# Transfers of keys and of split values in a top-k attention with two MoE layers: begun by ScalarE's queue in place of SyncE's

## The chip, the cores and the metric

The kernel runs on one core of a Trainium2 chip. The metric is the device time of one execution in microseconds; lower is better. Names of engines in the profile: PE is TensorE (PEld its weight loads), DVE is VectorE, ACT is ScalarE, POOL is GpSimd, and SPq is the queue of SyncE, which computes nothing and only begins transfers.

## What is computed

An attention that keeps the 32 largest scores of each row, and two MoE-like layers behind it, all in float32 accuracy.

```python
batch, n_heads, seq, head_dim = (4, 8, 576, 64)
scores = scale * np.matmul(q, k.transpose(0, 1, 3, 2))
kth = np.partition(scores, -top_k, axis=-1)[..., -top_k:-top_k + 1]   # top_k = 32
scores = np.where(scores >= kth, scores, -1000000000.0)
attn = softmax(scores)                                                 # + 1e-9 in the divisor
x = np.matmul(attn, v)            # to 2304 tokens x 512
x = (sigmoid(x @ w_gate) * (x @ w_val)) @ w_out      # 512 -> 1536 -> 512
out = np.maximum(x @ w_in, 0) ** 2 @ w_out2          # 512 -> 2048 -> 512
```

## The kernel before

The 2304 tokens are 18 tiles of 128 rows; `CHUNKS` makes 12 chunks of them: chunks 0 to 5 of one tile, chunks 6 to 11 of two. A sequence has 576 rows, so a tile can lie in two batches (then two key tiles are needed). Within a chunk the attention goes over four pairs of heads (`hp`), two heads (`j`) and the tiles (`i`); one such unit is: queries transposed, `scores` (L374, TensorE, into `sp`), a copy of them to SBUF by ScalarE (`S`, L377), four rounds of the eight largest by VectorE (L389, L396), the exponential by ScalarE (L408 to L424), and the product with the values.

For the accuracy, operands are split into a high and a low part. `prep_keys` reads the keys of a batch and a pair of heads, transposes them, casts the high part `kp` (L172, ScalarE), takes the low part `kn` (L173, VectorE) and stores both to a scratch tensor `ks` in HBM (L179, SyncE). `load_keys` (L326) fetches from there the 128 x 576 tile `kst` that a head needs; the pool has `KST` = 3 buffers for `kst`, and `kp` takes one of the same three. A buffer is free when the matmuls of the unit that read it are done.

From chunk 6 (`TCI`) on, values are split too: `prep_values` and `split_values` store them to the scratch `vd` (L229, L230), and `load` fetches `v` (L308) from it, into one of two buffers, free when the product `xp` of the earlier pair is done. Chunks 0 to 5 load plain values (L314, L317). From chunk 6 on the probabilities are transposed by a transfer, `PT<-S` (L456). Queries come by L298, outputs leave by L893. All these transfers are begun by SyncE, one after the other in one queue: an issue whose buffer isn't free holds up all that stand behind it.

The MoE layers of a chunk run on TensorE between the units of later chunks: pg and pv (L749), acc (L789), ph (L853), acc (L874). ScalarE, GpSimd and VectorE work on their results in between (th, gh, r, rh); the PSUM pool for pg, pv and ph has two buffers. For chunks 0 and 1 the same is done in float32 with lines of its own.

The order on every engine comes from a scheduler that gets the instructions with priorities (`tc.high_priority`, `at`, `attend`) and puts them in an order by its own plan of the time. The order is then fixed: each engine takes its instructions one by one and waits at each for what it needs. A change of one instruction's engine can therefore move others.

Of the kernel before, what the change touches and what calls it, by code (L numbers as in the profile page):

```python
# [10 lines left out]
F32 = mybir.dt.float32  # L11
# [33 lines left out]
XP = (0, 1)  # L45
CN = 16
CA2 = 5.0
SM2 = ()
XUP = 1000
DIAG = 2  # L50
# [24 lines left out]
def tile_topk_attention__then__two_moe_layers(  # L75
# [14 lines left out]
    nc = tc.nc  # L90
# [52 lines left out]
    kscr = {}  # L143
# [40 lines left out]
    vscr = {}  # L184
# [49 lines left out]
    def pieces(tt):  # L234
        r0, r1 = tt * P, (tt + 1) * P
        res = []
        while r0 < r1:
            b = r0 // S
            e = min(r1, (b + 1) * S)
            res.append((b, r0 - b * S, r0 - tt * P, e - r0))  # L240
            r0 = e
        return res
# [39 lines left out]
    class Pair:  # L282
# [9 lines left out]
        def load(self):  # L292
            ci, hp = self.ci, self.hp
            for tt in self.tts:
                qn = apool.tile([P, 2, 2, D], F32, tag="qn", bufs=2, name=f"qn_{tt}_{hp}")
                for b, s0, o, n in pieces(tt):
                    for a in range(2):
                        nc.sync.dma_start(  # L298
                            qn[o : o + n, :, a, :],
                            q[b, 2 * hp : 2 * hp + 2, s0 : s0 + n].rearrange("h p d -> p h d"),  # L300
                        )
                self.qt[tt] = qn
            for b, _, _ in self.segs:
                if ci >= TCI:
                    t = apool.tile(
                        [P, 2, 2, CB + 1, D], F16, tag="v", bufs=2, name=f"v_{ci}_{hp}_{b}"
                    )
                    nc.sync.dma_start(t, vscr[(b, hp)])  # L308
                    self.vt[b] = t
                    continue  # L310
                t = apool.tile([P, 2 * CB + 1, D], F32, tag="v", bufs=2, name=f"v_{ci}_{hp}_{b}")
                src = v[b, 2 * hp : 2 * hp + 2]
                for j in range(2):
                    nc.sync.dma_start(  # L314
                        t[:, j * CB : (j + 1) * CB], src[j, 0:SM].rearrange("(p c) d -> p c d", c=CB)
                    )
                    nc.sync.dma_start(t[j * ST : (j + 1) * ST, 2 * CB], src[j, SM:S])  # L317
                self.vt[b] = t

        def load_keys(self, j):  # L320
            h = 2 * self.hp + j
            if self.ci == 0:
                return
            for b, _, _ in self.segs:
                t = apool.tile([P, S], F32R, tag="kst", bufs=KST, name=f"kst_{self.ci}_{h}_{b}")
                nc.sync.dma_start(t.bitcast(F32), kscr[(b, h)].bitcast(F32))  # L326
                self.kt[(j, b)] = t

        def queries(self, tts):
# [676 lines left out]
    def attention():  # L1006
# [62 lines left out]
        def tail(n, after=None):  # L1069
# [3 lines left out]
            if pr.hp == 0 and pr.ci not in xts:  # L1073
# [10 lines left out]
                else:  # L1084

                    small = pr.ci in SM2
                    x = mpool.tile(
# [102 lines left out]
    for ci in PLAIN:  # L1190
        n = 0
        while True:
# [28 lines left out]
            else:  # L1221
                at(ta)
                with tc.high_priority(offset=0):
                    if next(att, 1) is None:
                        emitted[0] += 1
                ta += CA if emitted[0] < CN else CA2
        body = None
# [56 lines left out]
```

## Time and profile before

| | |
|---|---|
| median of three runs | 1276.93 us (1275.36 to 1278.46) |
| profiled execution | 1279.16 us |
| its span, first to last instruction | 1277.4 us |
| mean granted clock of TensorE | 0.955 of full speed |
| busy: PE, DVE, ACT, POOL | 93%, 75%, 65%, 66% |
| transfers of `kst` | 112 of 288 KB |
| transfers of split `v` | 32 of 320 KB |

A page and views of one profiled execution follow below as rows. A group of waits sums the idle time of an engine in front of an instruction by what ended it (the releaser, behind the arrow). A stretch gives the busy time of each engine in it, with the number of instructions in brackets. Busy time of an engine doesn't count the issuing of transfers. A granted clock of 1.00 is 2.4 GHz on TensorE, the lower level is 1.2 GHz; a mean between them says for what part of the stretch the lower one held.

### The profile page before, as it was taken

The numbers are of one execution on the slowest core, as the hardware profiler recorded it, in microseconds if no ns is written. First come the engines' busy times: TensorE is split into PE (matmuls) and PEld (weight loads), VectorE is DVE, ScalarE is ACT, GpSimd is POOL, SyncE is SP. The second block draws the span as 40 slices with busy tenths as digits, with TensorE's granted clock in tenths as the row PEclk, the third lists the DMA queues.
The fourth block names the chain that finished last, engine by engine and source line by source line (L and its number), as shares of the span: only waits on it lengthen the run. The fifth ranks groups of instructions, "written<-read, shape, count | busy, mean of one in ns | idle before, by whom it ended". The sixth has DMA issues, their size and how long they took to land.

```text
span 1277.4 us, 30680 instructions
## 1 busy us (share of the span) xinstructions
PE 1186.4 (93%) x11477; PEld 963.2 (75%) x11477; DVE 955.9 (75%) x1965; ACT 832.1 (65%) x1719; POOL 837.7 (66%) x1294
## 2 busy tenths in 40 slices
PE   6767989999889898999998999999999999999998
PEld 5556877987877877879786768877886887787775
DVE  6998888999778967889998779989989969210010
ACT  4998986677767666767777666777677757323122
POOL 1788864577766476787876877797778649515223
PEclk9567989999989998999998999999999999999999
DMA  7987862223344336765676656556444523200000
GB/s 189 352 301 258 272 193 77 75 79 84 103 131 125 104 80 144 143 151 115 143 135 158 119 131 143 129 113 162 105 82 96 120 48 67 55 1 1 17 1 18
DMA packets 243190, 153.94 MB, mean 121 GB/s; under 512 B 193120, under 2 KB 209504, under 8 KB 243040
## 3 DMA queue, kind: packets, MB, share of 16 engines
q1 hardware_dynamic: 243040, 151.97, 46.9%
q8 instruction: 91, 1.49, 0.5%
q14 instruction: 59, 0.48, 0.1%
HBM read 105.51 MB, written 18.09 MB: 97 GB/s over the span
## 4 chain that ended last, share of the span: by engine, by line
PE 64%; DVE 11%; DMA 8%; POOL 6%; ACT 5%; issue 3%; SPq 2%; POOLq 0%; DVEq 0%; ACTq 0%
PE ph L853 10%; PE acc L874 10%; PE pg L749 8%; PE pv L749 7%; PE acc L789 7%; PE sp L374 6%; DVE mx L389 5%; DVE W L396 4%; PE xp L506 3%; DMA PT<-S 3%; PE ph L954 2%; PE xp L533 2%; PE acc L971 2%; PE pg L907 2%; DMA kst<-ks 2%
## 5 line engine op out<-in xcount | busy, mean ns | idle before, releaser
L389 DVE MAX8 mx<-W 128x8 f32<-128x576 f32 x432 | 327.8, 759 | 10.8
L396 DVE MATCH_REPLACE8 W<-mx,W 128x576 f32<-128x576 f32 x288 | 213.8, 743 | 0.0
L853 PE MATMUL ph<-x,wi_w 128*128 128x256 f16 (+1 forms) x1920 | 193.0, 255 | 2.5 <-ACT x L827 1.9
L874 PE MATMUL acc<-w_w,rh 128*128 128x512 f16 x768 | 181.6, 379 | 3.2 <-POOL rh L866 3.1
L853 PEld LDWEIGHTS <-wi_w 128*128 128x128 f16 x1920 | 158.3, 100 | 29.1 <-issue 3.0
L749 PE MATMUL pg<-xs,wg_w 128*128 128x256 f16 (+1 forms) x1440 | 150.0, 256 | 3.5 <-ACT xs L520 2.8
L374 PE MATMUL sp<-kst,qt 128*128 128x288 f32 x608 | 135.7, 336 | 18.0 <-DMA kst<-ks 9.3
L749 PE MATMUL pv<-xs,wv_w 128*128 128x256 f16 (+1 forms) x1440 | 145.2, 254 | 4.8 <-DVE th L761 4.3
L377 ACT COPY S<-sp 128x576 f32<-128x576 f32 x144 | 91.9, 638 | 71.8 <-PE sp L374 42.5
L454 POOL TENSOR_TENSOR S<-W,S 128x512 f16<-128x512 f32 x192 | 136.7, 733 | 2.0
L749 PEld LDWEIGHTS <-wv_w 128*128 128x128 f16 x1440 | 118.7, 99 | 21.0 <-issue 8.4
L749 PEld LDWEIGHTS <-wg_w 128*128 128x128 f16 x1440 | 120.4, 100 | 18.4 <-issue 2.0
L408 ACT ACTIVATE W<-S,mx 128x576 f32<-128x576 f32 x144 | 111.6, 775 | 30.4 <-DVE mx L389 29.8
L874 PEld LDWEIGHTS <-rh 128*128 128x128 f16 x768 | 72.4, 98 | 75.4 <-POOL rh L866 4.0
L789 PEld LDWEIGHTS <-wo_w 128*128 128x128 f16 x1440 | 117.8, 98 | 13.6 <-issue 1.4
L761 DVE TENSOR_TENSOR th<-pv,th 128x512 f32<-128x512 f32 (+1 forms) x60 | 34.6, 577 | 121.5 <-PE pv L749 118.9
L389 DVE MAX8 mx<-S 128x8 f32<-128x576 f32 x144 | 107.3, 745 | 24.1 <-ACT S L377 24.1
L374 PEld LDWEIGHTS sp<-kst,qt 128*128 128x128 f32 x608 | 93.5, 198 | 29.3 <-DMA kst<-ks 9.7
L452 POOL TENSOR_SCALAR W<-W,rz 128x576 f32<-128x576 f32 x96 | 71.5, 745 | 66.8 <-ACT S L451 65.6
L865 POOL TENSOR_TENSOR r<-r 128x512 f32<-128x512 f32 (+1 forms) x80 | 69.5, 868 | 59.7 <-ACT rh L864 58.5
L396 DVE MATCH_REPLACE8 W<-mx,S 128x576 f32<-128x576 f32 x144 | 106.9, 742 | 0.0
L789 PE MATMUL acc<-gh,wo_w 128*128 128x256 f16 (+1 forms) x1104 | 105.0, 247 | 0.9 <-POOL gh L765 0.9
(290 smaller groups left out, 2324.1 us busy)
## 6 DMA issues: line engine op xcount, KB each, us to landing
kst<-ks SPq DMA_DIRECT2D x112, 288.0 KB, 3.1
v<-vd SPq DMA_DIRECT2D x32, 320.0 KB, 3.6
qn<-in_q_dram SPq DMA_DIRECT2D x128, 64.0 KB, 2.5
wi_r<-in_moe_w_in_dram SPq DMA_DIRECT2D x16, 512.0 KB, 6.5
w_r<-in_moe_w_out_dram SPq DMA_DIRECT2D x16, 512.0 KB, 5.2
v<-in_v_dram SPq DMA_DIRECT2D x56, 128.0 KB, 2.3
wg_r<-in_moe_w_gate_dram SPq DMA_DIRECT2D x12, 512.0 KB, 6.3
wv_r<-in_moe_w_val_dram SPq DMA_DIRECT2D x12, 512.0 KB, 6.8
```

Of the source, the lines that this page charges most:

```text
L374: nc.tensor.matmul(sp[:, e, 0:HALF], l, r, start=(x == 0), stop=(x == len(ops) - 1))
L377: nc.scalar.copy(ss.rearrange("p (e s) -> p e s", e=2), sp[:, :, 0:HALF])
L389: m8 = nc.vector.max(mx[:, r], cur)
L396: nc.vector.match_replace(wk, mx[:, r], cur, NEG)
L408: nc.scalar.activation(wk, ss, AF.Prelu, bias=kth, scale=-1.0, alpha=1.0 / BIG)
L452: nc.gpsimd.tensor_scalar(wk, wk, rz, 1.0, op0=ALU.mult, op1=ALU.mult)
L454: nc.gpsimd.tensor_tensor(pp[:, o : o + e - f], wk[:, f:e], pp[:, f:e], op=ALU.subtract)
L749: nc.tensor.matmul(pp[:, e * N : (e + 1) * N], wblk(wd, a, c, f0, P), xs[:, b_, c, :], start=(e == 0 and n == 0), stop=(n == 3 * KM - 1), ...
L789: nc.tensor.matmul(accs[d // 2][:, (d % 2) * N : (d % 2 + 1) * N], wblk("wo", a, f, d * P, P), gh[:, b_, e * N : (e + 1) * N], start=(f == ...
L853: nc.tensor.matmul(ph[:, e * N : (e + 1) * N], wblk("wi", a, c, f0, P), x2[:, b_, c, :], start=(e == 0 and n == 0), stop=(n == 3 * KM - 1) ...
L865: nc.gpsimd.tensor_tensor(r, r, r, op=ALU.mult)
L874: nc.tensor.matmul(acc2[i][:, 0:DM], gh[:, b_, e * N + i * P : e * N + (i + 1) * P], wblk("w2", a, f, 0, DM), start=(f == 0 and x == 0), s ...
```

## The change

Two constants choose the engine whose queue begins a transfer. With `VQ` = 1 all loads of split values (L308, 32 of them) are begun by ScalarE, with `KQ` = 4 the loads of keys from chunk index 4 on, the fifth chunk (88 of 112). The transfers themselves, their sizes and their buffers stay.

```diff
@@ -45,6 +45,8 @@
 XP = (0, 1)
 CN = 16
 CA2 = 5.0
+VQ = 1
+KQ = 4
 SM2 = ()
 XUP = 1000
 DIAG = 2
@@ -305,7 +307,7 @@
                     t = apool.tile(
                         [P, 2, 2, CB + 1, D], F16, tag="v", bufs=2, name=f"v_{ci}_{hp}_{b}"
                     )
-                    nc.sync.dma_start(t, vscr[(b, hp)])
+                    (nc.scalar if VQ else nc.sync).dma_start(t, vscr[(b, hp)])
                     self.vt[b] = t
                     continue
                 t = apool.tile([P, 2 * CB + 1, D], F32, tag="v", bufs=2, name=f"v_{ci}_{hp}_{b}")
@@ -323,7 +325,9 @@
                 return
             for b, _, _ in self.segs:
                 t = apool.tile([P, S], F32R, tag="kst", bufs=KST, name=f"kst_{self.ci}_{h}_{b}")
-                nc.sync.dma_start(t.bitcast(F32), kscr[(b, h)].bitcast(F32))
+                (nc.scalar if KQ and self.ci >= KQ else nc.sync).dma_start(
+                    t.bitcast(F32), kscr[(b, h)].bitcast(F32)
+                )
                 self.kt[(j, b)] = t
 
         def queries(self, tts):
```

The diff doesn't tell where these issues now stand. In the pieces below each row is a line, an operation, what it writes and reads, and its size; the lines after the change are 2 to 4 higher. The numbers in `kst_4_5_1` are chunk, head and batch; in `S_4_4` tile and head.

SyncE in the attention of chunk 4, before: the last loads of plain values of the pair, the stores of split values, and the keys.

```order
L314 DMA v_4_1_1_3446<-in_v_dram 128x256
L317 DMA v_4_1_1_3446<-in_v_dram 64x64
L229 DMA vd_1_1_3743<-vom_1_1_3676 128x2x256
L230 DMA vd_1_1_3743<-voe_1_1_3677 128x2x64
L229 DMA vd_1_1_3743<-vom_1_1_3676 128x2x256
L230 DMA vd_1_1_3743<-voe_1_1_3677 128x2x64
L197 DMA ve_1_2_4061<-in_v_dram 64x2x64 x2
L326 DMA kst_4_5_1_4087<-ks_1_2_1424 128x576
L326 DMA kst_4_6_0_4306<-ks_0_3_431 128x576
L326 DMA kst_4_6_1_4308<-ks_1_3_1889 128x576
L194 DMA vm_1_3_4491<-in_v_dram 128x256 x2
L326 DMA kst_4_7_0_4511<-ks_0_3_431 128x576
```

The same place after the change:

```order
L316 DMA v_4_1_1_3446<-in_v_dram 128x256
L319 DMA v_4_1_1_3446<-in_v_dram 64x64
L316 DMA v_4_1_1_3446<-in_v_dram 128x256
L319 DMA v_4_1_1_3446<-in_v_dram 64x64
L300 DMA qn_5_1_4778<-in_q_dram 128x2x64 x2
L231 DMA vd_1_2_4130<-vom_1_2_4064 128x2x256
L232 DMA vd_1_2_4130<-voe_1_2_4065 128x2x64
L231 DMA vd_1_2_4130<-vom_1_2_4064 128x2x256
L232 DMA vd_1_2_4130<-voe_1_2_4065 128x2x64
L199 DMA ve_1_3_4494<-in_v_dram 64x2x64 x2
L316 DMA v_4_2_0_3687<-in_v_dram 128x256
```

The four key transfers have left the queue; loads of values and stores now follow each other without them.

ScalarE at the copy of the scores of tile 4, head 4, before:

```order
L764 CAST gh_2_4_4222<-th_2_4_4218 128x256
L424 ACTIVATE W_4_2_3875,bs_4_2_3884<-W_4_2_3875,bs_4_2_3884 128x576
L541 COPY xt_4_3712<-xp_4_0_3853 128x128
L658 ACTIVATE w2_w5_3421<-w2_c5_1807,w2s_2082 128x1024
L377 COPY S_4_4_4089<-sp_4_4_4090 128x576
L759 ACTIVATE th_2_5_4299<-pg_2_5_4249,gsc_2_3505 128x256
L658 ACTIVATE w2_w6_3498<-w2_c6_1819,w2s_2082 128x1024
L764 CAST gh_2_5_4303<-th_2_5_4299 128x256
```

After the change, around the same copy `S_4_4`:

```order
L226 ACTIVATE vom_1_1_3676<-vm_1_1_3670,vsc_88 128x2x256
L226 ACTIVATE voe_1_1_3677<-ve_1_1_3673,vsc_88 128x2x64
L328 DMA kst_4_5_1_4087<-ks_1_2_1424 128x576
L381 COPY S_4_4_4089<-sp_4_4_4090 128x576
L328 DMA kst_4_6_0_4306<-ks_0_3_431 128x576
L768 CAST gh_2_3_4055<-th_2_3_4051 128x256
L763 ACTIVATE th_2_4_4218<-pg_2_4_4168,gsc_2_3505 128x256
L662 ACTIVATE w2_w4_3330<-w2_c4_1795,w2s_2082 128x1024
L412 ACTIVATE W_4_2_3875<-S_4_2_3701,mx_4_2_3876 128x576
L328 DMA kst_4_6_1_4308<-ks_1_3_1889 128x576
```

`kst_4_5_1` stands directly ahead of the copy and `kst_4_6_0` directly behind it; both take buffers that this tile's scores release. The steps around it changed places as well: `S_4_4` stood behind `gh_2_4` and now stands ahead of `gh_2_3`.

ScalarE at the first preparation of keys of batch 2, before:

```order
L172 CAST kp_2_0_6042<-kpt_2_0_0_6043 128x512
L819 ACTIVATE x2_3_5728<-acc1_3_0_5254 128x256
L172 CAST kp_2_0_6042<-kpt_2_0_4_6050 128x64
L819 ACTIVATE x2_3_5728<-acc1_3_1_5255 128x256
L408 ACTIVATE W_5_7_6083<-S_5_7_5888,mx_5_7_6084 128x576
L202 ACTIVATE voe_2_0_6032,vs_2_0_6033<-ve_2_0_6028 128x2x64
L424 ACTIVATE W_5_7_6083,bs_5_7_6111<-W_5_7_6083,bs_5_7_6111 128x576
L206 CAST vs_2_0_6033<-vs_2_0_6033 128x2
L475 COPY PT_5_6_6076<-tp_5_6_6077 128x512
L377 COPY S_6_1_6205<-sp_6_1_6206 128x576
L827 ACTIVATE x2_3_5728<-acc1_3_0_5254,x2s_3_5740 128x256
L827 ACTIVATE x2_3_5728<-acc1_3_1_5255,x2s_3_5740 128x256
```

After the change:

```order
L174 CAST kp_2_0_6042<-kpt_2_0_0_6043 128x512
L174 CAST kp_2_0_6042<-kpt_2_0_4_6050 128x64
L208 CAST vs_2_0_6033<-vs_2_0_6033 128x2
L328 DMA kst_6_1_1_6067<-ks_1_0_899 128x576
L412 ACTIVATE W_5_7_6083<-S_5_7_5888,mx_5_7_6084 128x576
L428 ACTIVATE W_5_7_6083,bs_5_7_6111<-W_5_7_6083,bs_5_7_6111 128x576
L831 ACTIVATE x2_3_5728<-acc1_3_0_5254,x2s_3_5740 128x256
L831 ACTIVATE x2_3_5728<-acc1_3_1_5255,x2s_3_5740 128x256
L479 COPY PT_5_6_6076<-tp_5_6_6077 128x512
L381 COPY S_6_1_6205<-sp_6_1_6206 128x576
L328 DMA kst_6_2_1_6203<-ks_1_1_1101 128x576
L226 ACTIVATE vom_2_0_6031<-vm_2_0_6025,vsc_88 128x2x256
```

Behind the two casts of `kp_2_0` and seven more steps of computing now stands the issue of `kst_6_2_1`. By the waits in that order, it waits for two of the stores of `ks_2_0` that SyncE begins, since it takes the buffer of `kp_2_0`. Of the 120 issues on ScalarE, 35 wait for scores, 32 for a product with values.

## Rows read from the trace of the kernel before

**Rows 1.** Part 1 of the page: engine, busy us, share, instructions
```profile
PE 1186.4 (93%) x11477; PEld 963.2 (75%) x11477; DVE 955.9 (75%) x1965; ACT 832.1 (65%) x1719; POOL 837.7 (66%) x1294
```

**Rows 2.** Stretches: length, busy PE, PEld, DVE, ACT, POOL, clock, DMA share, GB/s
```profile
400.00:500.00 100.00, 91.55 (x1182) 79.15 (x1180) 82.75 (x192) 68.02 (x163) 60.64 (x119) 0.93 0.44 112
...
800.00:900.00 100.00, 99.75 (x1027) 77.67 (x1026) 93.81 (x196) 71.81 (x151) 81.97 (x142) 1.00 0.58 132
```

**Rows 3.** Stretches of 20 us, the same columns
```profile
360.00:380.00 20.00, 15.90 (x171) 13.19 (x170) 15.70 (x39) 12.81 (x33) 9.89 (x22) 0.83 0.52 147
...
440.00:460.00 20.00, 17.52 (x187) 15.33 (x187) 16.41 (x42) 13.83 (x36) 10.38 (x21) 0.83 0.54 142
...
680.00:700.00 20.00, 15.82 (x133) 12.79 (x133) 18.29 (x43) 14.23 (x36) 13.22 (x23) 0.83 0.73 154
```

**Rows 4.** Waits of PE, 320 to 800 us: releaser, us in total, times, longest
```profile
PE sp L374 <- DMA kst<-ks: 9.3, 7, 2.9
...
PE sp L374 <- ACT S L451: 3.1, 1, 3.1
...
PE pg L749 <- ACT xs L520: 2.8, 1, 2.8
...
PE qpt L334 <- ACT qn L349: 0.2, 1, 0.2
```

**Rows 5.** Timeline of PE: start, us, instructions, idle before and releaser
```profile
363.55 1.35 PE L374 MATMUL sp<-kst,qt 128*128 128x288 f32 x6 [2.91 <-DMA kst<-ks]
...
445.05 0.79 PE L374 MATMUL sp<-kst,qt 128*128 128x288 f32 x4 [1.33 <-DMA kst<-ks]
...
794.59 1.06 PE L374 MATMUL sp<-kst,qt 128*128 128x288 f32 x6 [1.12 <-DMA kst<-ks]
```

**Rows 6.** Timeline of SyncE's queue before the first two of those
```profile
351.91 0.34 SPq L314 DMA_DIRECT2D v<-in_v_dram  x1
...
360.52 4.26 SPq L326 DMA_DIRECT2D kst<-ks  x3
...
439.99 0.33 SPq L308 DMA_DIRECT2D v<-vd  x1
...
441.01 0.59 SPq L326 DMA_DIRECT2D kst<-ks  x1
```

**Rows 7.** Timeline of ACT before the first of those
```profile
354.01 0.63 ACT L377 COPY S<-sp 128x576 f32<-128x576 f32 x1
```

**Rows 8.** Waits of SyncE's queue, 320 to 800 us
```profile
SPq L326 <- PE sp L374: 17.5, 14, 3.1
...
SPq L308 <- PE xp L506: 14.8, 4, 5.8
...
SPq L308 <- PE qpt L334: 9.9, 4, 6.0
```

**Rows 9.** Issues, 320 to 800 us, ns min/median/max; landing of L326
```profile
L326 SPq DMA_DIRECT2D kst<-ks x57: 319/379/1597, 319.7 to 795.8; - x57
...
DMA to landing us min/median/max: 2.7/3.2/4.5
...
L308 SPq DMA_DIRECT2D v<-vd x18: 319/354/1957, 440.0 to 799.6; - x18
```

**Rows 10.** Waits of ACT and of DVE, 320 to 800 us
```profile
ACT S L377 <- DMA PT<-S: 22.3, 14, 3.1
...
DVE mx L389 <- ACT S L377: 16.8, 8, 5.5
```

**Rows 11.** Preparation of keys: casts, the first's end, a store, landing of stores
```profile
L172 ACT CAST kp<-kpt x16: 212/404/592, 441.0 to 759.5; 128x512 fp32r<-128x512 f32 x8, 128x64 fp32r<-128x64 f32 x8
...
442.39 0.21 ACT L172 CAST kp<-kpt 128x64 fp32r<-128x64 f32 x1 [0.38 <-PE kpt L165]
...
444.21 1.23 SPq L179 DMA_DIRECT2D ks<-kn  x2
...
DMA to landing us min/median/max: 2.3/3.0/10.4
```

## The prediction

> **What bounds the kernel now.** I read the share of busy time first, then the span in stretches, then what TensorE itself waits for. TensorE is busy 93% of the span [rows 1]. That share hides two regimes. From 800 us on TensorE is full: 99.75 of 100 us in the first stretch of that part [rows 2], so whatever ScalarE or SyncE do there, on which the attention of the later chunks still runs, reaches the end only if it starves TensorE anew. Between 400 and 500 us it is busy 91.55 of 100 us and the granted clock is 0.93 [rows 2]. The change first acts in the attention of the fifth chunk, which begins a little after 300 us; so the time is decided between 320 and 800 us, by the idle time of TensorE there and by the clock that falls after some of it. A microsecond saved there is a microsecond of the end, since the dense part behind it only starts earlier.
>
> What TensorE waits for in that part: the largest row is the scores (L374) waiting for transfers of keys, 9.3 us in seven waits [rows 4], 2.91 us the longest [rows 5]. Thirteen rows of that view name ScalarE; the two largest are 3.1 and 2.8 us, the last is 0.2, and with those between they make 12.8 us in 16 waits [rows 4]. Three stretches of 20 us have a mean granted clock of 0.83 [rows 3]: at 1.2 of 2.4 GHz for a third of the stretch, which costs 0.17 x 20 = 3.4 us each. In the first two a wait for keys stands [rows 5].
>
> Why were the keys late? Follow SyncE's queue before the longest wait. The score of the unit before was copied out by ScalarE at 354.01 us [rows 7], so that unit's key buffer was free by then. But SyncE was at work on loads of plain values from 351.91 us, behind them came stores of split values and loads of value ends, without a gap, and the key transfers were begun at 360.52 [rows 6]: 6.5 us late, and TensorE stood 2.91 us. Before the wait at 445.05 SyncE stood at a load of split values that could begin only at 439.99, and the keys followed at 441.01 [rows 6]. So the keys were late in the queue, not in the transfer. All seven are of this kind: no idle time of SyncE directly ahead of the key's issue, only other issues.
>
> **The change part by part.** All of it against the profiled execution, 1279.16 us (span 1277.4); the median of the runs is 1276.93, 2.23 lower, and I subtract that at the end.
>
> *Waits for keys removed.* In the new order the key transfer stands on ScalarE directly beside the copy of the scores that frees its buffer, as the first pieces of order show. Begun at 354 instead of 360.5, the transfer, which lands in 3.2 us at the median [rows 9], is there before 360. I count 8 of the 9.3 us as saved, with 4 and 9.3 as bounds (some of the later waits had SyncE only 1 to 3 us behind).
>
> *Clock given back.* Two stretches at 0.83 hold a wait for keys [rows 3, 5]. Other idle time stands in them too, so I take one of the two, 3.4 us; bounds 0 and 6.8.
>
> *SyncE relieved.* It loses 57 key transfers and 18 of split values in this part [rows 9], and with them waits of 17.5 us for scores, and of 14.8 and 9.9 us for buffers of split values [rows 8]. Behind those stood the transposes of the probabilities (L456), and ScalarE waits 22.3 us for these before it may overwrite S, and VectorE 16.8 us for S in turn [rows 10]. Little of that reached TensorE: the first matmul of a MoE stage waited 2.8 us for attention at 682 us [rows 4], in the third stretch at 0.83 [rows 3]. I take 2 us; bounds 0 and 2.8 + 3.4 = 6.2.
>
> *ScalarE loaded.* An issue takes SyncE 379 ns for keys and 354 ns for values at the median [rows 9]. The trace has none on ScalarE. If it costs the same there, it is 57 x 0.379 + 18 x 0.354 = 28.0 us in a part in which ScalarE is about 70% busy (68.02 of 100 us from 400 on [rows 2]). Most falls into its idle time. TensorE feels it where it already waits for ScalarE: 16 waits, each lengthened by one issue, are 6.1 us; half of them have an issue ahead of them at this density, so 3.2 us. Bounds: 0, if ScalarE's queue runs an issue beside its datapath, and 28. A gain is excluded, as ScalarE loses no work.
>
> *New waits on ScalarE.* 67 of the 120 issues wait for TensorE: 35 for scores, 32 for the product with values (L506, L533). Nearly all stand next to a copy on ScalarE that needs that same result, so ScalarE would have stood there anyway; I count nothing. If that cover fails, what is queued behind is th, gh and r of the MoE, and the price is in the rival below. Different is the group at the preparation of keys (third pieces of order): there kst takes a buffer that the hi part kp has just used, and ScalarE must wait until SyncE's stores of it have landed. There are eight such preparations between 441 and 760 us (16 casts, two each [rows 11]). In the first, the cast ended near 442.6, the last store was begun near 444.8 and takes 3.0 us at the median [rows 11], so landing is at 447.8. In the new order seven steps of ScalarE, some 4 us, stand between cast and issue: it gets there near 446.7 and stands about 1 us. I take 1.5 us each, 12 us of ScalarE's time, a fifth of it felt by TensorE: 2.5 us. Bounds 0 and 8 x 3.0 = 24.
>
> Sum: -8 - 3.4 - 2 + 3.2 + 2.5 = -7.7. 1279.16 - 7.7 - 2.23 = **1269.2**, I say 1269.
>
> A rule speaks against this. What the rows show: before the keys of 360.52 an unbroken run of issues of 8.6 us on SyncE, where a transfer itself lands in 3.2 [rows 6, 9]. The Trainium skill, "DMA: Bandwidth & Descriptors", section "Issuing engines are not separate DMA queues", says that transfers begun by several engines run on the same 16 DMA engines and that only the issue time is saved, usually small beside the transfer. The trace agrees that the issue time is what is saved, and disagrees that it is small here. What it would give is the third rival.
>
> **The rivals.**
> *ScalarE stands where TensorE needs it (slower).* At the eight preparations ScalarE waits for stores on another engine's queue. Were SyncE held up behind a transpose there, the stall would be 3 us and not 1.5, and th and r of the MoE queue behind it; the MoE stages have two PSUM buffers for them, so TensorE soon stands too. 8 x 3.0 = 24 us instead of 2.5: 1276.93 - 13.4 + 3.2 + 24 = 1291; 1294 if the clock's 3.4 do not come back either. It turns the sign from (13.4 - 3.2) / 8 = 1.3 us of TensorE per preparation. For it: the stores really stand in the same queue as the transposes. Against: SyncE is emptier. Half of that price, 12 us, gives 1279 and already ends a little on the slow side.
> *The wait moves (no change).* TensorE works in a fixed order and VectorE is itself at 82.75 of 100 us from 400 on and 93.81 from 800 on [rows 2]. Keys that come earlier may only bring TensorE to the next wait sooner, for S, th or rh. Then most of the 13.4 is lost and the 5.7 is left: half of the gain kept gives 1276.93 - 6.7 + 5.7 = 1276.
> *Only one issue is saved per wait.* If the transfers queue just as long elsewhere, each of the seven waits shrinks by one issue: 7 x 0.38 = 2.7. 1276.93 - 2.7 + 5.7 = 1280, slower by 0.23%. That is what the Trainium skill's rule would give. Against it: the DMA engines are at 0.44 of their time from 400 to 500 us [rows 2].
> *The change does not do what it says:* excluded for the issues, which stand on ScalarE. But the planner moved rows on every engine from the end of the fourth chunk's attention on: attention of chunk 4 now stands earlier among the MoE matmuls, that of later chunks a little later. That makes and removes waits that no row prices; it widens the range.
>
> **How the numbers follow.** Forecast 1269: 0.52. Slower by ScalarE's stalls: 0.20. The wait moves: 0.18. One issue saved: 0.10. A measurement of this kernel can tell 0.2%, 2.6 us, from no change: faster means under 1274.4, slower above 1279.5. The forecast is on the fast side but for little; of the second rival a fifth is. Faster 0.55, same 0.18, slower 0.27. Range: down to all gains whole without a cost, 9.3 + 6.8 + 6.2 = 22.3, which is 1254.6; I say 1256. Upward to where most of the slow rival is in: 1286. The forecast's own range is 1256 to 1275.
>
> **What would show it.** Right: TensorE's waits for kst between 320 and 800 under 2 us; the stretches of 20 us around 363 and 445 at clock 1.00; ScalarE's waits ahead of S and xs for TensorE no longer than now; SyncE's waits at L326 and L308 gone. Wrong: ScalarE with rows of idle time at the new issues that end at stores of keys, by more than 1.5 us each; TensorE's waits for ScalarE above 20 us instead of 12.8; or kst waits as long as before, with their issues now late on ScalarE.

## The result: 0.72% slower

The changed kernel takes 1282.61 us (median of 7 executions, 1281.11 to 1288.79), the kernel before, run beside it, 1275.36. The ratio taken from all these runs (not from the two medians, which give 1.0057) is 1.0072, with a 95% interval of 1.0053 to 1.0092. I forecast 1269, a gain of 0.6%; the sign is wrong.

The profiled execution of the changed kernel took 1287.75 us (span 1285.9), 5.1 above the median of its runs; that of the kernel before lay 2 to 5 us above the medians of its runs. Lines of the code stand 2 lower up to the load of keys and 4 lower behind it: L152 is now L154, L308 is L310, L326 is L328, L456 is L460. TensorE's row, the stretches from 400 to 900 us and, last, the sum of the same five stretches of the kernel before:

```profile
PE 1185.4 (92%) x11477; PEld 962.3 (75%) x11477; DVE 957.6 (74%) x1965; ACT 830.6 (65%) x1719; POOL 844.1 (66%) x1294
```
```profile
400.00:500.00 100.00, 90.49 (x1245) 78.07 (x1243) 81.29 (x188) 66.61 (x161) 61.40 (x120) 0.98 0.43 105
500.00:600.00 100.00, 91.62 (x1240) 79.32 (x1238) 83.86 (x192) 68.30 (x161) 72.73 (x135) 0.97 0.64 133
600.00:700.00 100.00, 90.38 (x920) 73.20 (x918) 89.37 (x189) 66.63 (x149) 70.30 (x122) 0.97 0.66 138
700.00:800.00 100.00, 96.40 (x884) 73.91 (x882) 78.31 (x168) 67.12 (x147) 78.41 (x127) 1.00 0.57 129
800.00:900.00 100.00, 95.60 (x927) 73.44 (x927) 92.56 (x193) 68.74 (x147) 79.24 (x137) 0.97 0.66 132
sum 500.00, PE 464.49 PEld 377.94 DVE 425.38 ACT 337.40 POOL 362.08; mean PE 92.90 PEld 75.59 DVE 85.08 ACT 67.48 POOL 72.42
```
```profile
sum 500.00, PE 474.84 PEld 388.08 DVE 434.22 ACT 347.71 POOL 369.82; mean PE 94.97 PEld 77.62 DVE 86.84 ACT 69.54 POOL 73.96
```

TensorE has the same work [rows 1], but is busy 10.3 us less between 400 and 900 us. It isn't the clock: its mean over these five stretches is 0.98 in both kernels. Even the stretch from 800 on, which was full at 99.75 [rows 2], has 4.4 us of idle time. What TensorE waits for, 320 to 800 us (releaser, us in total, times, longest), beside [rows 4]:

```profile
PE kpt L167 <- DMA kn<-in_k_dram: 7.9, 4, 2.8
PE sp L378 <- DMA kst<-ks: 7.0, 4, 3.8
PE sp L378 <- ACT S L381: 3.6, 5, 1.1
PE xp L537 <- ACT PT L479: 3.5, 2, 2.2
PE xp L510 <- DMA PT<-S: 2.6, 2, 1.9
PE ph L857 <- ACT x L831: 2.2, 1, 2.2
```

The waits for kst went from 9.3 to 7.0 us. New at the top are the loads of raw keys (kn), 3.6 us in three waits before, and the products that wait for a transpose (PT<-S), which had 0.4 us before. Neither of these transfers was moved by the change. The two moved ones, and then the landing of the transposes, which SyncE begins as ever (the first line of the third fence is the changed kernel, 320 to 1060 us, the second the kernel before):

```profile
L328 ACTq DMA_DIRECT2D kst<-ks x54: 326/327/1254, 325.0 to 796.0; - x54
```
```profile
L310 ACTq DMA_DIRECT2D v<-vd x17: 326/326/343, 438.7 to 783.3; - x17
```
```profile
DMA to landing us min/median/max: 3.2/3.7/8.5
...
DMA to landing us min/median/max: 3.2/3.3/6.2
```

An issue takes ScalarE's queue 0.33 us, less than it took SyncE's (0.38 and 0.35 at the median [rows 9]). The transposes land later.

### The profile page after: what moved, and what is told of

The parts are those of the page before. It is cut to its first block, busy times and chain, and to the rows that moved or that the text cites. A ratio compares the mean times of both kernels' runs of the same rounds, so it can differ in the third digit from the quotient of the medians.

```text
span 1285.9 us, 30671 instructions
## 1 busy us (share of the span) xinstructions
PE 1185.4 (92%) x11477; PEld 962.3 (75%) x11477; DVE 957.6 (74%) x1965; ACT 830.6 (65%) x1719; POOL 844.1 (66%) x1294
## 4 chain that ended last, share of the span: by engine, by line
PE 58%; DVE 16%; DMA 8%; POOL 7%; ACT 5%; issue 3%; SPq 2%; ACTq 0%; DVEq 0%; POOLq 0%
PE ph L857 10%; PE acc L878 9%; PE acc L793 7%; DVE mx L393 7%; PE pg L753 6%; PE pv L753 6%; DVE W L400 6%; PE sp L378 5%; DMA PT<-S 3%; PE xp L510 3%; PE ph L958 2%; PE acc L975 2%; PE pg L911 2%; PE xp L537 2%; DMA vd<-vom 2%
## 5 line engine op out<-in xcount | busy, mean ns | idle before, releaser
L857 PE MATMUL ph<-x,wi_w 128*128 128x256 f16 (+1 forms) x1920 | 189.8, 254 | 4.2 <-ACT x L831 3.8
L455 ACT ACTIVATE S<-W,rz 128x576 f16<-128x576 f32 x96 | 74.3, 774 | 51.9 <-DVE rz L451 45.3
```

What stands on the lines that cost most here:

```text
L455: nc.scalar.activation(pp[:, 0:S], wk, AF.Copy, scale=rz)
L857: nc.tensor.matmul(ph[:, e * N : (e + 1) * N], wblk("wi", a, c, f0, P), x2[:, b_, c, :], start=(e == 0 and n == 0), stop=(n == 3 * KM - 1) ...
```

## The experiments

Two things changed at once: the queue, and the order that the scheduler gives to all engines. To take them apart I wrote an order out and held it with ordering edges between neighbours on each engine:

```diff
         tile_topk_attention__then__two_moe_layers(tc, *args)
+        _pin(nc, tc)
+def _pin(nc, tc):
...
+    for e, *d in json.loads(zlib.decompress(base64.b85decode("".join(_ORDER)))):
...
+            tc.add_manual_dep(i, last, info, reason="order")
```

Kernels that differ only in queues can then be laid over each other, instruction by instruction.

### The queue alone, the order alone, values alone, keys alone

```diff
 VQ = 1
-KQ = 4
+KQ = 0
```

is the run of values alone; VQ = 0 and KQ = 4 that of keys alone (both with an order worked out anew).

> The 120 transfers are begun by ScalarE, each right behind the ScalarE instruction that stands ahead of it in the program order before, and the instructions of every engine keep the order that they had before (the order is written out and fixed by ordering edges between neighbours; TensorE, VectorE and GpSimd have the very sequence of before). Theory O (the new order of all engines cost the time; begun by ScalarE alone, the transfers do what the prediction said): the time is below that of before by about the predicted 7.7 us, 1266 to 1272 us, and at most equal to it; the waits for kst in 320 to 800 us fall from 9.3 us to under 4. Theory Q (the second queue itself costs it: transfers on two queues land later, ScalarE stands at its new issues): slower than before by the 7 us of the change, 1280 to 1285 us, with the transposes' landing at 3.7 us and the stores of vd at 2.7 us as in the changed kernel. Between them, 1274 to 1278 us, the queue is worth nothing either way.

> All 120 transfers are begun by SyncE again, at their place in the changed kernel's program order, and every engine has the order of the changed kernel. Theory O: as slow as the changed kernel, 1280 to 1285 us, or slower still by the waits for keys that SyncE's queue then brings back (up to 1290); the landing of the transposes goes back to 3.3 us all the same, so that it is not the cause. Theory Q: back to the kernel before, 1273 to 1278 us.

> Only the 32 transfers of split values are begun by ScalarE; the keys stay with SyncE. The program's order is worked out anew and differs from before in some rows from about 500 us on. Theory Q, by count: 32 of 120 transfers, a quarter of the loss, 1277 us. Theory O: what the new order is worth, which the count doesn't tell: anywhere in 1268 to 1284, and without relation to the sum with the run of keys alone.

> Only the 88 transfers of keys from the fifth chunk on are begun by ScalarE; split values stay with SyncE. Theory Q, by count: three quarters of the loss, 1281 us, and with the run of values alone it adds up to the change's 7 us. Theory O: what this order is worth, anywhere in 1268 to 1286; since up to about 640 us its order is that of the changed kernel, the stretches up to there lose what the changed kernel lost there (PE idle in 300 to 640 us longer than before by some 5 us).

Measured against the kernel before: queue alone 1.0041 (1.0026 to 1.0056), order alone 1.0025 (1.0009 to 1.0041), values alone 1.0056 (1.0039 to 1.0072), keys alone 1.0028 (1.0012 to 1.0043). The first two fall into the ranges of theory Q (1280.64 and 1277.71 us), but neither theory has it all: queue and order each cost something, the queue perhaps more (the intervals overlap). And 32 values cost no less than 88 keys, so, as far as the new orders of these two runs allow the comparison, the number of issues is not what counts.

In the queue run each of TensorE's 11,477 matmuls has its twin in the kernel before. I subtracted the starts of the twins: the run is 1.05 us later at 620 us of the kernel before, 3.60 at 640, 8.61 at 683, 9.90 at 760 and 7.05 from 860 to the end. (It is 4.2 us ahead at 500. I took that for a gain of the keys; a run below, in which no key moves, is 2.8 us ahead at 500 and 4.1 at 540. The profiled execution of the kernel before, 1279.16, is 2 to 5 us above the medians of its runs, so most of the 4 us lies in that one execution. That of the queue run, 1286.85, is the slowest of its twelve, 6.2 above their median. So the places are what can be read from this, not the size of the loss.) Two steps, of 2.3 and 3.8 us, stand out. The larger one stands at 661.72 of the kernel before, 669.18 of this run. SyncE's queue, ScalarE, the landing of that one transpose, and TensorE in the queue run:

```profile
659.06 1.29 SPq L460 DMA_TRANSPOSE PT<-S  x1
665.42 1.29 SPq L154 DMA_DIRECT2D kn<-in_k_dram  x2
```
```profile
659.09 0.34 ACTq L310 DMA_DIRECT2D v<-vd  x1
```
```profile
DMA to landing us min/median/max: 6.3/6.3/6.3
```
```profile
669.18 1.09 PE L167 MATMUL kpt<-ident,kn 128*128 128x128 f32 x4 [3.68 <-DMA kn<-in_k_dram]
```

The same place on SyncE's queue in the kernel before:

```profile
654.72 1.30 SPq L456 DMA_TRANSPOSE PT<-S  x1
656.12 0.53 SPq L308 DMA_DIRECT2D v<-vd  x1
658.02 1.31 SPq L152 DMA_DIRECT2D kn<-in_k_dram  x2
```

On one queue the load of split values could only begin behind the transpose's 1.30 us of issue; the transpose landed after 3.2 us, and kn, whose buffer (it is one of the five of S) the transpose gives free, began at 658.02, 3.30 us behind the transpose's start. The load itself, in line behind it, took 4.45 us. With a queue of its own the same load begins 0.03 us behind the transpose and lands after 3.53. The transpose lands after 6.3 us, kn begins 6.36 us behind it, and TensorE stands for 3.68 us. Then the clock falls: 0.83 in the 20 us from 664 on, where the kernel before had 1.00 from 660 on (two stretches of the queue run, then one of the kernel before). The kernel before has such a fall 20 us later, 0.83 from 680 on [rows 3], where the queue run has 0.91 from 684 on. So part of this fall is that one come earlier.

```profile
664.00:684.00 20.00, 16.32 (x143) 13.30 (x142) 12.85 (x29) 11.15 (x27) 11.57 (x21) 0.83 0.66 154
684.00:704.00 20.00, 14.79 (x127) 11.64 (x126) 17.40 (x40) 12.25 (x29) 11.53 (x20) 0.91 0.61 109
```
```profile
660.00:680.00 20.00, 17.91 (x192) 15.10 (x190) 16.43 (x38) 13.85 (x29) 12.07 (x22) 1.00 0.74 168
```

The second place, 622 us: v and kst begun by ScalarE at 622.30 and 623.44, a transpose begun at 621.61 that lands after 7.5 us, and ScalarE, which must wait for it before it may write S again:

```profile
622.30 0.64 ACTq L310 DMA_DIRECT2D v<-vd  x1
622.99 0.78 ACT L455 ACTIVATE S<-W,rz 128x576 f16<-128x576 f32 x1 [0.33 <-DVE rz L451]
623.44 0.33 ACTq L328 DMA_DIRECT2D kst<-ks  x1
629.18 0.64 ACT L381 COPY S<-sp 128x576 f32<-128x576 f32 x1 [5.41 <-DMA PT<-S]
```
```profile
631.88 0.39 PE L878 MATMUL acc<-w_w,rh 128*128 128x512 f16 x1 [2.17 <-ACT rh L868]
```

The MoE's rh stands behind that copy on ScalarE, so TensorE stands for 2.17 us in the middle of a MoE stage.

That gives a theory (T below): a transfer of 288 or 320 KB begun on a second queue while a transpose is being issued holds the transpose up. Over all transposes from 300 us on in the queue run: 47 with no such transfer then or in the 3 us before land after 3.48 us in the mean, 20 that have one within 1.3 us behind their start after 5.17. In the changed kernel it is 22, at 5.15.

The twins tell how much of that is due to the second queue. The same 20 transposes landed after 3.96 us in the mean in the kernel before, 10 of them after more than 4; the other 76 went from 3.64 to 3.69. So the hit ones, slower than the rest from the start, became slower by 1.2 us each, and the rest hardly at all. One queue is no full protection either: in the kernel before 17 transposes have a key or value transfer begun 1.2 to 1.6 us behind them on SyncE, and none in the 3 us ahead. 14 of these land within 3.7 us, three after 4.5 to 4.9; their mean is 3.53. And a key or value transfer begun in the 3 us ahead of a transpose costs as much on one queue (38 transposes in the kernel before, 4.01) as on two (29 without a hit in the queue run, 4.05). What is new on two queues is the transfer that begins right behind.

### Taking the hits away, and only them

In the queue run 23 of the 120 transfers were begun from 0.6 us ahead of a transpose's start to 1.25 us behind it. A list of numbers decides which transfer stands where:

```diff
-                    (nc.scalar if VQ else nc.sync).dma_start(t, vscr[(b, hp)])
+                    _queue(nc).dma_start(t, vscr[(b, hp)])
...
+def _queue(nc):
+    _CALLS.append(0)
+    return nc.scalar if len(_CALLS) - 1 in _ON_ACT else nc.sync
```

> As the run with the queue alone (order of before on every engine), but the 23 transfers that ScalarE began in that run from 0.6 us ahead of a transpose's start on SyncE to 1.25 us behind it are left with SyncE, at their old place; 97 stay with ScalarE. Theory T (a key or value transfer begun on a second queue while a transpose is being issued makes the transpose land at 4.4 to 7.5 us in place of 3.3, and the S buffers, kn loads and xp products that wait for the transposes come late): the transposes over 5 us go from 14 back to about 6, their median to 3.3 us, and the time falls from the queue run's 1280.6 to that of before, 1274.5, or to the 4 us under it that the queue run had gained by 500 us: 1270 to 1275. Theory A (ScalarE stands at its new issues, or the issues share completion semaphores with SyncE's): 97 of 120 issues are still there, so four fifths of the loss of 6 us stays, 1278 to 1281.

> The complement: only those 23 transfers are begun by ScalarE, the other 97 stay with SyncE; order of before on every engine. Theory T: the loss is in them, 1278 to 1283, with the transposes over 5 us at about 14. Theory A: one fifth of the loss, 1275 to 1276.

> Only the 32 transfers that ScalarE began before 500 us in the queue run (the keys of the fifth and sixth chunk, and what of values lies there) are begun by it; order of before on every engine. In the queue run TensorE's instructions were 4.2 us earlier than in before at 500 us, and later by 7 us only behind that, where the transposes were hit. Theory T: 1270 to 1272, a gain. Theory A: each issue costs, 32 of 120 of the loss, 1276.

> The changed kernel with its own order on every engine, but the 32 transfers that it began on ScalarE from 0.6 us ahead of a transpose's start to 1.25 us behind it are put back on SyncE; 88 stay with ScalarE. Theory T: the changed kernel's 1282.6 falls to the order-only run's 1277.7 or a little under it, 1274 to 1278, since what stays is the new order and the earlier keys. Theory A: 88 of 120 issues, 1281.

Measured: the 97 others on ScalarE 1.0019 (1.0000 to 1.0039); the 23 alone **1.0070** (1.0045 to 1.0096); the first 32 alone 0.9996 (0.9978 to 1.0013); the changed kernel with its 32 hits put back 0.9984 (0.9965 to 1.0003). So 23 transfers cost as much as the whole change, and no less than all 120 in the same order (1.0041); putting 32 back takes the changed kernel from 1.0072 to 0.9984, 0.9% or 11 us. Theory A, a price per issue, gave the 23 a fifth of the loss; it falls. In the run of the 23 the place of above repeats itself, with the load of v 0.35 us behind the transpose's start (landing, SyncE, TensorE):

```profile
DMA to landing us min/median/max: 6.2/6.2/6.2
```
```profile
658.27 1.30 SPq L460 DMA_TRANSPOSE PT<-S  x1
664.54 1.30 SPq L154 DMA_DIRECT2D kn<-in_k_dram  x2
```
```profile
668.14 1.09 PE L167 MATMUL kpt<-ident,kn 128*128 128x128 f32 x4 [3.17 <-DMA kn<-in_k_dram]
```

The 23 alone, at 1285.24 us, cost even more than theory T said. Two expectations failed. The 97 took 1278.05, not the 1270 to 1275 of theory T, and 12 of their transposes land after more than 5 us, where I expected about 6: 11 other transfers had come to stand beside a transpose. And the first 32, in which I saw a gain of 4 us, gain nothing. In that run TensorE's waits for kst are no shorter than before:

```profile
PE sp L378 <- DMA kst<-ks: 10.7, 9, 2.1
```

### Bytes or issue, later in the queue, and the search for a gain

> As the run with the queue alone (order of before on PE, VectorE and GpSimd; 119 of the 120 transfers begun by ScalarE), but 22 of the 23 transfers that hit a transpose stand 1 to 5 rows further back in ScalarE's order, behind the first instruction that began at least 1.35 us after the transpose's start, so that they are begun when the transpose's issue is over; one, whose place would fall behind its own reader, stays with SyncE. Theory T (being begun during the transpose's issue is what costs): transposes over 5 us at 6 to 9, time 1273 to 1278, like the run with the 23 left on SyncE (1.0019). Rival P (these 23 are dear because ScalarE begins just these, whenever it does): as the run of the 23 alone or the whole queue, 1280 to 1286.

> The kernel before with its order on every engine and all 120 transfers with SyncE; in addition ScalarE begins 23 transfers of 64 bytes (into a tile that nobody reads) at the very places at which the run of the 23 alone had its key and value transfers. Theory B (the bytes of a second transfer share the way with the transpose's): transposes stay at their 3.3 us median with 6 over 5 us, time as before, 1274 to 1277. Theory I (any second issue during a transpose's issue, or ScalarE's own time for it, costs): transposes that have one behind them at over 4.4 us, time 1280 to 1285.

> As the run with 97 transfers on ScalarE, but the 11 that in that run newly fell into a transpose's issue are left with SyncE too; 86 stay with ScalarE, order of before. Theory T: what that run still lost goes as well: 1270 to 1275, at or under the kernel before. If the keys begun earlier are worth nothing by themselves (as the run of the first 32 says, 0.9996), 1274 to 1277 and no better than before.

> The changed kernel's order on every engine. All 32 transfers of split values are begun by SyncE again, and the keys that hit a transpose in the changed kernel or in the run without those hits too; 71 keys stay with ScalarE. Theory T: values of 320 KB are the larger hits, and some that ScalarE began a little over 0.6 us ahead of a transpose still slowed it (4.6 to 5.3 us) in the run that left only the 32 hits to SyncE; without them the transposes over 5 us fall from 9 to about 6 and the time is at or under that run's 1273.6 (0.9984 of before): 1271 to 1274. If SyncE's queue is what matters there, values that stand on it again cost what the order-only run lost: 1276 to 1278.

The edit of the first moves rows of ScalarE's order and gives one transfer back to SyncE; that of the second, beside the transfer that stays with SyncE:

```diff
                     nc.sync.dma_start(t, vscr[(b, hp)])
+                    _tiny(nc, dm, k)
...
+        _TINY.append(nc.scalar.dma_start(dm[n : n + 1, 0:16], k[0, 0, 0:1, 0:16]))
```

The other two change the list of numbers.

*64 bytes in place of 288 or 320 KB:* 0.9992 (0.9977 to 1.0008), no loss. Of the 23 small transfers 19 were begun between 0.6 us ahead of a transpose's start and 1.3 us behind it, as the large ones were. The profile of this run has no landing times, but ScalarE tells them at the second place of above. Its small transfer begins 0.65 us behind the transpose's start at 616.68 (the large one: 0.69), and the copy into S waits 1.94 us for the transpose, where it was 5.41:

```profile
617.33 0.22 ACTq L1309 DMA_DIRECT2D dm<-in_k_dram  x1
617.89 0.78 ACT L457 ACTIVATE S<-W,rz 128x576 f16<-128x576 f32 x1 [0.15 <-DVE rz L453]
620.61 0.64 ACT L383 COPY S<-sp 128x576 f32<-128x576 f32 x1 [1.94 <-DMA PT<-S]
```

So it is neither ScalarE's own time for an issue nor a second issue as such (theory I falls). What costs is what the transfer moves, as theory B says: its bytes, or the number of its packets, which no run separates from them.

*Off twice* (86 on ScalarE, order of before): 1.0006 (0.9989 to 1.0023), no loss and no gain. At the place of above the transpose lands after 3.2 us again.

*Pushed back on ScalarE* (119 there): 1.0034 (1.0019 to 1.0048). Its median of 1279.83 us is above the 1273 to 1278 of theory T and just under the 1280 to 1286 of rival P, and it doesn't differ from the queue run by more than the intervals. So the time of this run doesn't exclude rival P; what speaks against P is the trace. In its trace eight transposes have a transfer begun within 1.3 us behind their start after all, since everything shifted; one of them lands after 8.9 us. At the two places of above TensorE loses 1.5 and 2.8 us against its twins, where it lost 2.3 and 3.8 in the queue run. Where the push did as meant, at 654.25, the transpose lands after 4.9 us, between 3.2 and 6.3: the load of v, now begun 2.80 us behind its start, still meets it on the way. On SyncE's own queue the same load, begun 1.40 us behind, left the transpose at 3.2 us. So theory T's window, the issue, is too narrow. As far as three runs of this one place tell (the load begun 0.03, 0.35 and 2.80 us behind, landing after 6.3, 6.2 and 4.9), two queues that carry both at once cost the transpose, and less the later the second begins.

*All values and the hits back on SyncE* (71 keys on ScalarE, order of the changed kernel): 1.0020 (0.9999 to 1.0041), where I expected under 1274 us. Its transposes are the best of all (4 over 5 us), but they were read in an execution of 1272.97 us, 5.2 under the median of its runs (1278.13); those of the run with 88 (9 over 5 us) in one of 1282.38, 8.8 above its median (1273.63). So these two counts say little of a usual execution. The time lies at the second branch of my expectation, that fewer transfers on ScalarE bring back what SyncE's queue costs in this order (order alone 1.0025), but no run shows that cause. No run beats the kernel before by more than its interval; the best is the one with 88 transfers on ScalarE at 0.9984.

The table holds all runs but the one with 64 bytes, which has no landing times (landings in us from one profiled execution each, transposes from 300 us on; "hit" is a transpose with a key or value transfer of the other queue begun within 1.3 us behind its start; the third column is the mean of the transposes with neither a hit nor a key or value transfer of either queue begun in the 3 us before; "over 5 us" counts all 96):

| run | hits, mean landing | others | over 5 us | ratio |
|---|---|---|---|---|
| before | 0 | 3.50 | 6 | 1 |
| changed | 22, 5.15 | 3.64 | 15 | 1.0072 |
| queue alone | 20, 5.17 | 3.48 | 14 | 1.0041 |
| order alone | 0 | 3.64 | 8 | 1.0025 |
| values alone | 9, 5.72 | 3.49 | 17 | 1.0056 |
| keys alone | 11, 4.65 | 3.51 | 6 | 1.0028 |
| 97 without the hits | 8, 5.46 | 3.47 | 12 | 1.0019 |
| the 23 hits alone | 14, 4.94 | 3.51 | 13 | 1.0070 |
| first 32 | 1, 5.10 | 3.48 | 8 | 0.9996 |
| changed, 32 hits back | 2, 3.45 | 3.66 | 9 | 0.9984 |
| pushed back | 8, 5.46 | 3.48 | 10 | 1.0034 |
| off twice | 3, 3.76 | 3.54 | 7 | 1.0006 |
| 71 keys | 0 | 3.67 | 4 | 1.0020 |

The four runs with 13 or more transposes over 5 us are the four with the largest loss. Below that the order of the rows is not that of the ratios. That it matters which transposes are hit, and that the hits differ between executions, is my guess at why; each row has one execution only.

## Why the prediction was wrong, step by step

*What bounds the kernel:* right in the main. The time was lost between 400 and 900 us as idle time of TensorE, so not only up to 800, and not by the clock.

*Waits for keys removed, -8:* wrong in the sum, which is 7.0 in place of 9.3 us in the changed kernel, 9.2 in the queue run, 10.7 with the first 32. At the places it was nearly right, for another reason. The scores (L374) come in the same sequence in both kernels, so they can be compared one by one. Of the seven that waited for keys five no longer do, with 7.6 of the 9.3 us; the one that waited 2.91 us at 363.55 [rows 5] begins at 346.86 without a wait. But the queue didn't do that: in the run with the order alone, where SyncE begins all keys, this wait is gone too, and in the queue run, where the order is that of before, it is still 1.79. I wrote that the transfer would be "begun at 354 instead of 360.5". In the queue run it is begun at 359.46, because on ScalarE the issue stands in line as well, behind work that waits for TensorE (changed kernel; then the queue run's ScalarE and TensorE):

```profile
346.86 1.04 PE L378 MATMUL sp<-kst,qt 128*128 128x288 f32 x6
```
```profile
359.45 0.38 ACT L823 ACTIVATE x<-acc 128x256 bf16<-128x256 f32 x1 [1.24 <-PE acc L793]
359.46 0.33 ACTq L328 DMA_DIRECT2D kst<-ks  x1
```
```profile
362.56 1.06 PE L378 MATMUL sp<-kst,qt 128*128 128x288 f32 x6 [1.79 <-DMA kst<-ks]
```

What the sum got back stands at other scores of the changed kernel: 0.95 us at 364.73, 0.7 more at 330.0, and 3.80 at 482.46:

```profile
482.46 0.79 PE L378 MATMUL sp<-kst,qt 128*128 128x288 f32 x4 [3.80 <-DMA kst<-ks]
```

Its kst transfer was begun at 477.20, 0.5 us ahead of a transpose, and landed after 5.21 us: the key transfers, too, pay for the company. But this score had waited 3.07 us before as well, for ScalarE (the row of S L451 in [rows 4]). There the wait moved, as the second rival says.

*Clock given back, -3.4:* about right. The stretch from 440 on went from 0.83 to 1.00, that from 360 on stayed at 0.83, that from 680 on is at 0.91 [rows 3]. Between 320 and 800 us the mean went up (before, then changed):

```profile
320.00:800.00 480.00, 444.26 (x5225) 369.84 (x5223) 400.26 (x880) 330.68 (x756) 345.82 (x612) 0.96 0.56 128
320.00:800.00 480.00, 438.75 (x5186) 364.40 (x5184) 394.07 (x865) 325.25 (x746) 346.28 (x604) 0.98 0.55 125
```

With three places these are 0.964 and 0.975; times 480 us the lower level cost 17.1 us and then 11.9. Of the 5.2 us 3.3 were lost again from 800 to 900, at 0.97 in place of 1.00.

*SyncE relieved, -2:* the failed step, with the wrong sign. I reasoned that the transposes stood behind the key transfers on SyncE and would come sooner. They do start without them ahead, but what stood behind a transpose on the queue had kept off its way while it was issued. The order of one queue was a priority. Taking the keys and values out of it cost the transposes 0.4 us at the median and 2.3 us at the longest (3.3 to 3.7, 6.2 to 8.5; with the order alone 3.4 and 6.1). TensorE felt it as waits for kn, whose buffers the transposes give free: 3.6 us before, 7.9 in the changed kernel, 9.3 in the queue run, 4.7 with the order alone. The term had given them no price. (The waits in xp, 0.4 to 2.6, belong to the order: with it alone they are 3.4, in the queue run 0.6.) The wait that it did name, ScalarE's 22.3 us for transposes [rows 10], fell to 14.7 in the changed kernel and 17.6 with the order alone, but rose to 30.9 in the queue run.

*ScalarE loaded, +3.2:* too high. An issue took 327 ns on ScalarE's queue and ran beside its datapath (above, 359.46 beside 359.45): the lower of my bounds, 0, holds as far as the run with 23 tiny issues of 0.22 us can tell. Half of 6.1 is also 3.05 and not 3.2, which would have made the forecast 0.15 us lower.

*New waits at the key preparations, +2.5:* too high. ScalarE's idle time that the profile puts down to stores of keys sums to 3.3 us in three waits, 2.0 the longest, against the 12 that I put in. TensorE's waits for ScalarE, in which both of these terms would show, are 14.7 us between 320 and 800, against 12.8.

*The rivals.* That ScalarE stands, 1291 or more, did not happen. That the wait moves, 1276, and that one issue is saved per wait, 1280, both have a part of the truth in the keys term: the gain was lost. Neither has the transposes. That 1280 comes near the measured 1282.61 is luck: its loss is the 5.7 us of the two ScalarE terms, which measured far less. The Trainium skill, "DMA: Bandwidth & Descriptors", section "Issuing engines are not separate DMA queues", says that transfers begun by several engines run on the same 16 DMA engines. The runs fit that: 320 KB on ScalarE's queue held up a transpose on SyncE's by 3.0 us, and 64 bytes at such places cost the program nothing. I used the sentence to price a missing gain and not to ask whom the transfers would meet.

*The new order of all engines,* to which I gave no price: 1.0025 by itself, though it removes the longest wait for keys, and no loss (0.9984) with the queue for which it was planned, once the hits are out. Why it needs that queue I did not settle.

## What to carry to other kernels

Before a transfer goes to a second queue, list what its old queue held it behind. A short transfer with a long chain hanging on it (here a transpose that frees a score buffer) is mostly protected by the queue from the large ones behind it, and loses that when they get a queue of their own. Move the transfers that don't fall beside it, or leave them; and hold the order fixed when you measure a queue, or the scheduler's new order is measured with it.

## What was not expected of the hardware

- The 20 transposes of the queue run beside which ScalarE began 288 or 320 KB within 1.3 us behind their start landed after 5.17 us in the mean, 3.96 in the kernel before; the other 76 after 3.69 and 3.64. With 64 bytes in the same places the program lost nothing.
- An issue on ScalarE costs its queue 0.33 us and its datapath nothing that shows; on SyncE it was 0.35 to 0.38 [rows 9].
- Loads suffer as well: in the queue run the two loads of value ends (ve) at 359 us landed after 3.3 and 3.6 us beside key transfers on the other queue, 2.1 and 2.2 without them. TensorE gained 1.1 us at the keys there, and stood 1.84 us for the values' sums behind ve 3 us later.
